# One row of w2 per partition, loaded early in four uneven transfers, in a decode block on one Trainium2 core

## The chip, the core and the metric

The kernel runs on one core of a Trainium2 chip. The core has five engines, each with its own instruction stream: TensorE (PE, with PEld for its weight loads), VectorE (DVE), ScalarE (ACT), GpSimd (POOL) and SyncE (SP), and 16 DMA engines that carry bytes from HBM into SBUF. The metric is the device time of one launch in microseconds (us).

## The reference

Two tokens (B = 2, one each) of width D = 512 pass through an attention part and a feed-forward part, both modulated by a condition `c`:

```python
mod = (_silu(c) @ w_mod).reshape(c.shape[0], 6, 1, -1)
sa, ca, ga, sb, cb, gb = (mod[:, 0], ..., mod[:, 5])
h = _layernorm(x) * (1 + ca) + sa
x = x + ga * _A_ref(h, k_cache, v_cache, wq, wo)   # 32 query heads, 8 KV heads, the last 4096 positions
h = _layernorm(x) * (1 + cb) + sb
x = x + gb * _B_ref(h, w1, w2)                     # silu(h @ w1) @ w2, w1 512x1792, w2 1792x512
```

Everything is float32. The last line's second product, `silu(...) @ w2`, is what the change touches.

## The kernel before, in words

All large inputs are streamed once from HBM into three buffers (`slot[0..2]`, 16384 floats per partition each) by loads on SyncE's queue, in this order: `w_mod`, `wq`, then the four K and four V pieces of the caches alternately, then `wo` in two loads, `w1` in one, and `w2` in four. A load starts as soon as the buffer it writes has been given free; the instructions are put down once, in program order, and a helper (`Flow`) adds the semaphore waits from the regions that instructions read and write. All instructions therefore stand under one line, L117, in the profile. Each load has a semaphore of its own. On each DMA engine the packets of one queue are worked off in the order in which the loads were issued.

`w2` has 1792 rows of 512. Partition p holds rows 14p to 14p+13 (T2 = 14), so "row q" below means 128 rows of the matrix, one per partition, 2 KB in each. `load_rows` loads rows lo to hi of every partition in one transfer: rows 0-7 (2048 KB), 8-11 (1024 KB), 12 and 13 (256 KB each).

The end of the kernel (lines 672 to 713): 64 products make the hidden layer in two halves; VectorE and ScalarE turn each half into `uT` (transpose, scale, silu). Then follow, on TensorE:

- the wide products: rows 0-7, each one product over all 512 columns, four side by side in the partitions of bank D (`product`); ScalarE copies the sum to `wide`;
- the narrow products: for each further row, four products of 128 columns into `y` (`narrow`), rows 8-11; then the copied wide sum, added through `id4` by the same helper; then rows 12 and 13.

VectorE scales `y` by `gb` and adds `x1`, and SyncE stores the result.

## Time and profile before

| | us |
|---|---|
| median of 3 runs (lowest, highest) | 234.55 (234.53, 234.64) |
| the profiled execution, its own time | 234.44 |
| its span, first to last instruction | 233.1 |
| busy: PE, DVE, ACT, POOL | 161.0, 107.5, 32.5, 7.3 |
| bytes read | 97.53 MB, 418 GB/s over the span |

The span is shorter than the time by what lies before the first and after the last instruction. A row of the timeline gives start, length, engine, line, operation, output<-inputs, form and count, and in brackets the idle time before it with what ended it. The chain of work that ended last goes back from the last instruction, at each step to what released it. For a load, the time from its issue to its landing is given; issue plus that time is when an engine waiting for it can go on. The DMA share is the mean busy share of the 16 DMA engines: one engine alone is 0.06.

### The profile page before, as it was taken

The page shows a single profiled execution, that of the slowest core. Times are in us where ns is not written, and L with a number is a line of the kernel's source. Part 1 is how long each engine was busy: PE and PEld are TensorE (multiplying, and loading weights), DVE is VectorE, ACT ScalarE, POOL GpSimd, SP SyncE. Part 2 cuts the span into 40 slices and gives each one's busy share as a digit, 9 for nine tenths or more (in the row PEclk, how much of TensorE's full clock was granted, in tenths as well). Part 3 has the DMA queues.
Part 4 walks back from the last instruction along what each step waited for, and adds up shares of the span by engine and source line. Part 5 has one row for each costly group of instructions (what it writes and reads, how often), then busy time and mean ns, then how long its engine had stood idle before and what let it go on. Part 6 is the DMA issues. An engine that isn't in the chain of part 4 may idle for free.

```text
span 233.1 us, 2459 instructions
## 1 busy us (share of the span) xinstructions
PE 161.0 (69%) x1086; PEld 43.8 (19%) x1086; DVE 107.5 (46%) x137; ACT 32.5 (14%) x57; POOL 7.3 (3%) x26
## 2 busy tenths in 40 slices
PE   0013906920699479989669989829998937989965
PEld 0002201210000011023300023310002422543332
DVE  6014130131999699833099924049965010020351
ACT  2003010010000244021400021140003050010501
POOL 4000000000000000000000000000000030000000
PEclk9999985775599979999979999988999997999999
DMA  7998998989989898899989999899998989989992
GB/s 270 473 518 360 416 484 360 531 371 472 416 371 529 371 507 374 382 506 394 498 371 416 472 405 486 382 472 416 405 475 382 507 354 413 498 346 442 421 403 90
DMA packets 2494, 97.68 MB, mean 419 GB/s; under 512 B 284, under 2 KB 308, under 8 KB 564
## 3 DMA queue, kind: packets, MB, share of 16 engines
q1 hardware_dynamic: 2460, 97.52, 97.2%
q8 instruction: 8, 0.13, 0.2%
q14 instruction: 2, 0.02, 0.0%
q10 hardware_dynamic: 24, 0.01, 0.0%
HBM read 97.53 MB, written 0.00 MB: 418 GB/s over the span
## 4 chain that ended last, share of the span: by engine, by line
DMA 49%; DVE 26%; PE 19%; another core or an unknown queue 3%; issue 1%; ACT 1%; SPq 0%; POOL 0%
DVE store L117 24%; DMA store<-in_A_k_cache_dram 17%; DMA store<-in_B_w_dram 16%; DMA store<-in_A_wq_dram 15%; PE bankD L117 13%; PE bankA L117 3%; DVE mx L117 2%; PE bankC L117 1%; PE bankO L117 1%; PE bankB L117 1%; ACT store L117 1%; SPq L117 0%; DVE qbd L117 0%; DVE mg L117 0%
## 5 line engine op out<-in xcount | busy, mean ns | idle before, releaser
L117 DVE STREAM_TRANSPOSE store<-store 128x2048 f32<-128x2048 f32 (+2 forms) x40 | 77.1, 1981 | 33.6 <-DMA store<-in_A_k_cache_dram 27.9
L117 PE MATMUL bankA<-store,qbd 128*16 128x512 f32 x256 | 64.5, 1082 | 24.6 <-DVE store L117 23.0
L117 PE MATMUL bankD<-store,ptb 128*32 128x256 f32 (+1 forms) x384 | 45.0, 461 | 4.2 <-DMA store<-in_A_v_cache_dram 4.2
L117 PE MATMUL bankD<-store 128*32 128x512 f32 x176 | 23.2, 677 | 10.0 <-DMA store<-in_A_wq_dram 8.0
L117 PEld LDWEIGHTS bankD<-store,ptb 128*32 128x32 f32 (+1 forms) x384 | 17.3, 121 | 32.6 <-issue 24.1
L117 PE MATMUL bankB<-store 128*32 128x256 f32 (+3 forms) x72 | 7.2, 471 | 20.6 <-DVE store L117 20.6
L117 PEld LDWEIGHTS bankA<-store,qbd 128*16 128x16 f32 x256 | 4.6, 97 | 76.4 <-DVE store L117 75.9
L117 ACT COPY bias<-bankB 128x1 f32<-128x1 f32 x4 | 0.6, 159 | 85.7 <-PE bankB L117 85.7
L117 PEld LDWEIGHTS bankD<-store 128*32 128x32 f32 x176 | 6.8, 124 | 25.6 <-issue 22.1
L117 ACT ACTIVATE ptb<-bankC,par 128x512 f32<-128x512 f32 x16 | 11.0, 688 | 3.1 <-PE bankC L117 2.7
L117 ACT COPY store<-bankD 128x512 f32<-128x512 f32 (+1 forms) x7 | 3.9, 558 | 48.8 <-PE bankD L117 48.8
L117 DVE TENSOR_REDUCE mx<-bankA 128x1 f32<-128x1024 f32 x4 | 4.9, 1225 | 8.7 <-PE bankA L117 8.7
L117 PEld LDWEIGHTS bankB<-store 128*32 128x32 f32 (+1 forms) x72 | 3.9, 149 | 24.1 <-DVE store L117 22.2
L117 DVE RECIPROCAL store<-bankB 128x2 f32<-128x2 f32 x1 | 0.2, 171 | 17.1 <-PE bankB L117 17.1
L117 POOL MEMSET store<- 128x128 f32 (+3 forms) x11 | 3.2, 293 | 137.9 <-PE bankD L117 118.2
L117 PE MATMUL bankC<-qbd,store 128*128 128x512 f32 x14 | 7.3, 626 | 0.0
L117 DVE STREAM_TRANSPOSE store<-bankD 128x512 f32<-128x512 f32 x2 | 1.4, 720 | 12.1 <-PE bankD L117 12.1
L117 DVE STREAM_TRANSPOSE store<-bankA 128x128 f32<-128x128 f32 (+1 forms) x2 | 0.7, 368 | 12.3 <-PE bankA L117 12.3
L117 PE MATMUL bankO<-store,pick 128*64 128x128 f32 x32 | 4.4, 279 | 2.9 <-ACT store L117 2.9
L117 ACT ACT_TABLE_LOAD x4 | 5.1, 1283 | 2.8 <-DVE id L117 2.8
L117 ACT ACTIVATE store<-store,key 128x512 f32<-128x512 f32 x7 | 4.7, 716 | 5.5 <-DVE store L117 5.5
L117 DVE BATCH_NORM_STATS2 store<-x_sp 128x6 f32<-128x128 f32 x1 | 0.3, 295 | 10.7 <-DMA x_sp<-in_A_x_dram 10.7
(79 smaller groups left out, 61.4 us busy)
## 6 DMA issues: line engine op xcount, KB each, us to landing
store<-in_w_mod_dram SPq DMA_DIRECT2D x1, 6144.0 KB, 17.1
store<-in_A_wo_dram SPq DMA_DIRECT2D x1, 6144.0 KB, 33.6
store<-in_B_w_dram SPq DMA_DIRECT2D x1, 3584.0 KB, 31.9
store<-in_A_wo_dram SPq DMA_DIRECT2D x1, 2048.0 KB, 38.1
store<-in_B_w_dram SPq DMA_DIRECT2D x1, 2048.0 KB, 36.5
store<-in_B_w_dram SPq DMA_DIRECT2D x1, 1024.0 KB, 38.5
store<-in_B_w_dram SPq DMA_DIRECT2D x2, 256.0 KB, 38.7
store<-in_A_k_cache_dram SPq DMA_DIRECT2D x4, 33.5
```

What stands on the lines that cost most here:

```text
L117: ins = getattr(eng, method)(*args, **kw)
```

## The change

The last row of each partition (row 13) is no longer the last load. It is loaded right behind `w1`, ahead of all other rows of `w2`, in four transfers that take the partitions 0-50, 51-75, 76-79 and 80-127. The other loads become rows 0-7, 8-10, 11 and 12. The products follow the new order: row 13 comes first among the narrow ones, straight behind the wide products, then rows 8-10, the wide sum, and rows 11 and 12. Their number stays the same.

```diff
     w1t |= load_rows(w1, 4, 0, 4, slot[0], 0)
-    for lo, hi in ((0, 8), (8, 12), (12, 13), (13, 14)):
+
+    w2t[T2 - 1] = slot[0][:, 4 * F + (T2 - 1) * D :][:, :D]
+    for p0, p1 in ((0, 51), (51, 76), (76, 80), (80, P)):
+        sp.dma_start(
+            w2t[T2 - 1][p0:p1], w2.rearrange("(p q) e -> p q e", q=T2)[p0:p1, T2 - 1]
+        )
+    for lo, hi in ((0, 8), (8, 11), (11, 12), (12, 13)):
         w2t |= load_rows(w2, T2, lo, hi, slot[0], 4 * F + lo * D)
...
     act.copy(wide, acc)
-    for tt in range(8, T2 - 2):
-        narrow(y, uT[:, tt, :], w2t[tt], tt == 8, False)
+    narrow(y, uT[:, T2 - 1, :], w2t[T2 - 1], True, False)
+    for tt in range(8, T2 - 3):
+        narrow(y, uT[:, tt, :], w2t[tt], False, False)
     narrow(y, id4, wide, False, False)
-    for tt in range(T2 - 2, T2):
-        narrow(y, uT[:, tt, :], w2t[tt], False, tt == T2 - 1)
+    for tt in range(T2 - 3, T2 - 1):
+        narrow(y, uT[:, tt, :], w2t[tt], False, tt == T2 - 2)
```

## The prediction, made before the changed kernel ran

> **What bounds the kernel now.** I read the page first (span, queues), then the chain of work that ended last, then the timeline of the last 12 us, then the SyncE queue's issues, and last the DMA share in slices of 0.2 us. The page says that one queue moves nearly all bytes and is busy for nearly the whole span:

> ```profile
> span 233.1 us, 2459 instructions
> q1 hardware_dynamic: 2460, 97.52, 97.2%
> q8 instruction: 8, 0.13, 0.2%
> q14 instruction: 2, 0.02, 0.0%
> q10 hardware_dynamic: 24, 0.01, 0.0%
> ```

> The columns after the queue's name are packets, MB and share of 16 engines' span. The kernel is a stream of loads; what an edit at its end can win is only how soon the last arithmetic follows the last bytes. The chain (start, length, what) shows that end:

> ```profile
> 190.38 38.46 DMA store<-in_B_w_dram
> 228.84 0.04 issue
> 228.88 1.78 PE bankA L117 x56
> 230.66 0.02 issue
> 230.69 0.30 DVE store L117
> ```

> The load issued at 190.38 (w2 rows 8-11) lands at 228.84; TensorE then runs 56 instructions with no further wait on the chain, and 2.4 us of fixed work (two VectorE instructions, the store) follow to 233.1. Which landings matter is seen by putting the issues beside their times to landing:

> ```profile
> 189.53 0.33 SPq L117 DMA_DIRECT2D store<-in_B_w_dram  x1
> 189.90 0.91 SPq L117 DMA_DIRECT2D store<-in_B_w_dram  x2
> 190.86 0.46 SPq L117 DMA_DIRECT2D store<-in_B_w_dram  x1
> 191.36 1.11 SPq L117 DMA_DIRECT2D store<-in_B_w_dram  x1
> store<-in_B_w_dram SPq DMA_DIRECT2D x1, 3584.0 KB, 31.9
> store<-in_B_w_dram SPq DMA_DIRECT2D x1, 2048.0 KB, 36.5
> store<-in_B_w_dram SPq DMA_DIRECT2D x1, 256.0 KB, 38.6
> store<-in_B_w_dram SPq DMA_DIRECT2D x1, 256.0 KB, 38.7
> ```

> So w1 lands at 189.53+31.9 = 221.4, rows 0-7 at 189.90+36.5 = 226.4, row 12 at 190.86+38.6 = 229.46, row 13 at 191.36+38.7 = 230.06. TensorE against these:

> ```profile
> 225.22 0.18 DVE L117 TENSOR_TENSOR store<-store 128x14 f32<-128x14 f32 x1
> 226.49 2.03 PE L117 MATMUL bankD<-store 128*32 128x512 f32 x16 [1.73 <-DVE store L117]
> 227.24 0.18 DVE L117 TENSOR_TENSOR store<-store 128x14 f32<-128x14 f32 x1
> 228.56 0.59 ACT L117 COPY store<-bankD 128x512 f32<-128x512 f32 x1 [1.84 <-PE bankD L117]
> 228.88 1.08 PE L117 MATMUL bankA<-store 128*32 128x128 f32 x32 [0.36 <-DMA store<-in_B_w_dram]
> 229.78 0.40 PE L117 MATMUL bankA<-store,id 128*32 128x128 f32 x8
> 230.00 0.62 PE L117 MATMUL bankA<-store 128*32 128x128 f32 x16
> ```

> The wide products start at 226.49. The trace names VectorE as their releaser, but its instruction was over at 225.40; what ended last is the landing of rows 0-7 at 226.4. Then TensorE stands for 0.36 us until rows 8-11 are there. Row 13 lands at 230.06, before TensorE reaches it (its 8 instructions are the last of the 16 from 230.00), so the very last transfer isn't what ends the kernel: **two waits do, 226.4 for rows 0-7 and 228.84 for rows 8-11**.

> The third thing is how evenly the 16 engines finish (columns: window, its length, busy time of PE, PEld, DVE, ACT and POOL with counts, clock, DMA share, GB/s):

> ```profile
> 227.50:227.70 0.20, 0.20 (x8) 0.11 (x2) 0.00 (x0) 0.00 (x0) 0.00 (x0) 1.00 1.00 399
> 227.70:227.90 0.20, 0.20 (x7) 0.00 (x0) 0.00 (x0) 0.00 (x0) 0.00 (x0) 1.00 0.63 246
> 227.90:228.10 0.20, 0.20 (x8) 0.00 (x0) 0.00 (x0) 0.00 (x0) 0.00 (x0) 1.00 0.52 195
> 228.30:228.50 0.20, 0.20 (x4) 0.00 (x0) 0.00 (x0) 0.00 (x0) 0.00 (x0) 1.00 0.66 256
> 228.70:228.90 0.20, 0.02 (x3) 0.02 (x3) 0.00 (x0) 0.20 (x1) 0.00 (x0) 1.00 0.54 205
> 228.90:229.10 0.20, 0.20 (x8) 0.20 (x12) 0.00 (x0) 0.20 (x1) 0.00 (x0) 1.00 0.53 205
> 229.10:229.30 0.20, 0.20 (x16) 0.20 (x12) 0.00 (x0) 0.05 (x1) 0.00 (x0) 1.00 0.35 133
> 229.30:229.50 0.20, 0.20 (x18) 0.20 (x12) 0.00 (x0) 0.00 (x0) 0.00 (x0) 1.00 0.17 62
> q8 instruction: 1, 0.02, 10.6%
> q14 instruction: 1, 0.01, 1.0%
> ```

> All 16 are busy until 227.7; about 10 (0.66) at 228.4, 8 or 9 (0.53) at 229.0, none soon after 229.5. So six engines are through at about 227.8, a couple at about 228.7, eight between 229.1 and 229.5. The last two rows say why: one code fetch (q8) in a window of 0.6 us held 10.6% of 16 engines, 1.02 us of one engine, and there are eight of them; one q14 packet in a window of 2 us held 1.0%, 0.32 us, and there are two. Eight engines late by 1.3 to 1.7 us, two by less, six by nothing: the counts fit.

> **The change part by part.** *How four odd transfers are spread.* The queue rows can be counted out: 2460 = 17 loads x (128 rows + 16 completions) + 12 for the store, and 24 = 2 x (8 rows + 4 completions) for the two loads whose outermost dimension is 4. A load over 128 goes to 16 engines in shares of 8, one over 4 to four engines in shares of 2; every row that there is shows equal shares. For 51, 25, 4 and 48 partitions no row exists. The ends are 3, 5, 4 and 16 engines (equal shares: 51 = 3x17, 25 = 5x5) and, at the other end, nearly 16 each. I take equal shares, the only kind in the rows, and that each load begins at the same first engine: three engines get 17+5+1+3 = 26 rows, the fourth 9, the fifth 8, eleven get 3 (78+9+8+33 = 128), where each had 8. [...] By unequal shares the sum would be that of the even rival below.

> *Price of a 2 KB row on one engine:* eight rows per engine lie between 229.46 and 230.06: 0.60/8 = 0.075; between rows 8-11 and row 12, 0.62/8 = 0.078. I take 0.077.

> *What moves.* Row 13 (all 128 partitions) now sits ahead of rows 0-7 in every engine's queue. Rows 0-7 come later by 3 x 0.077 = 0.23 us on eleven engines and by 26 x 0.077 = 2.0 us on three. At the end of the stream the eleven are 5 x 0.077 = 0.39 us earlier, the three 18 x 0.077 = 1.39 us later. w1 stands ahead of all this and keeps 221.4.

> *TensorE.* 14 rows of products before and after, the same instruction count; row 13's eight now come straight behind the wide products, with no wait since it landed long ago, and cover the 0.36 us gap. From the start of the wide products the work is 2.03+1.78 = 3.81 us if nothing overlaps; it is less, since consecutive groups overlap (the group at 229.78 starts 0.18 before the one before it ends at 229.96) and the second half of the wide products needs a VectorE result of 227.42, past which they now start. I use 3.5, with 3.8 as the other end.

> *Waits and issues.* Three more loads on SyncE's queue cost it 0.33 to 1.11 us each; behind them stand only later loads, needed some 37 us on, and the output store after TensorE's end, so that is the cover. Row 13 needs four waits on TensorE instead of one; its instructions queue behind wide products of 2.03 us, which hide them (by the chain's 0.04 us after a landing, 0.16 us uncovered). The copy of the wide sum (0.59 us) has four rows' products between it and its use, as before; they took 1.08-0.18 = 0.90 us, so it stays hidden though they now start with it.

> *The sum* hangs on which three engines are first. If one of them is of the middle group (0.8 us ahead of the last), it has rows 0-7 at about 226.4-0.8+2.0 = 227.6, and the wide products start at 227.7. End of TensorE 227.7+3.5 = 231.2 (3.8: 231.5) instead of 230.66: +0.54 to +0.84; I take +0.6, near the end that the overlap shows. Rows 8-10 (three quarters of 2.44 us, 1.83) land at 229.4, row 12 at 230.7, both just ahead of need. The profiled execution took 234.44 us, 0.11 under the median shown: 234.44+0.6 = 235.04, and 235.1 on the median's scale.

> **Rivals.**
> *Clean three (not slower).* All three are of the six: rows 0-7 land there at 226.4-1.7+2.0 = 226.7, on the eleven at 226.63; start 226.8, end 230.3 to 230.6: -0.36 to -0.06, so 234.2 to 234.5. It decides once the three are 1.7 us ahead. For it: six such engines exist. Against: no view names an engine; followed packet by packet (each starts as its predecessor on that engine ends), two of the four engines that carried ScalarE's small loads seem to have had the q14 packets. That tilts me to the middle group. No more than this can be won: every engine gets three rows ahead of rows 0-7.

> *Even spread (the change does nothing of its kind).* Eight rows on each engine: rows 0-7 at 226.4+0.62 = 227.0, start 227.1, end 230.6 to 230.9: 0 to +0.25, 234.5. Against: equal shares in the counts.

> *A late engine among the three.* One of the eight that had a 1.02 us fetch: rows 0-7 at 226.0 to 226.4+2.0, start 228.1 to 228.5, end 231.6 to 232.0: +0.95 to +1.35, 235.5 to 236.0. By mere count likely (eight of 16); against it the same tracking.

> *Shared write path.* A 26-row share covers at least 18 partitions that other engines write at the same moment with their own loads. If a partition's path takes one engine's rate, such a row costs up to twice: 18 x 0.077 = 1.39 us more at most, half of it 0.7. On top of the forecast +1.3 to +2.0, so 235.8 to 236.5. In the trace 16 engines never cross: no row shows it either way. [...]

> **How the numbers follow.** Forecast 0.38, clean 0.20, even 0.12, late engine 0.16, shared path 0.14. Bounds of 0.2% (0.47 us) are about what a measurement here can tell. Faster by that needs more than the clean case's -0.36: 0.06, for what I may have missed. Same: the rest of clean (0.14), even (0.12), the forecast's lower edge (0.14): 0.40. Slower: 0.24+0.16+0.14 = 0.54. The range runs from 234.1 (clean) to 236.2, leaving out part of the shared path; the forecast's own is 234.8 to 235.4.

> **What would show it.** Wide products later than 226.49 (227.7 by the forecast, 226.8 if clean) show the three's load; narrow work right behind them, without a 0.36 us gap, shows the cover. DMA share: eleven engines done 0.4 us earlier and three left alone past 229.6 (0.19 of 16) is the forecast; a sharp common end is the clean case; packets of 2 KB much over 0.077 us in 219 to 223 the shared path. The prediction is wrong if the wide products start before 226.9 or after 228.1.

## The result, and the profile after

The changed kernel takes 237.06 us (median of 6 runs, 236.20 to 237.77) against 234.60 before: ratio 1.0105, interval 1.0085 to 1.0124. It is slower, by more than the 235.1 forecast and beyond the range's 236.2. The six times lie at two levels, 236.20 to 236.44 and 237.69 to 237.77, three each. The profiled execution is one of the upper ones (237.76 us).

From the page of the changed kernel, its span and the queue that carries the loads:

```profile
span 236.4 us, 2465 instructions
q1 hardware_dynamic: 2616, 97.52, 96.6%
```

Its chain of waits (start, length, what):

```profile
191.56 37.09 DMA store<-in_B_w_dram
228.66 0.14 issue
228.79 3.52 PE bankD L117 x16
232.31 1.61 PE bankA L117 x56
```

And the last part of its timeline:

```profile
222.57 1.74 PE L117 MATMUL bankA<-store 128*32 128x224 f32 x32 [1.28 <-DMA store<-in_B_w_dram]
228.31 0.18 DVE L117 TENSOR_TENSOR store<-store 128x14 f32<-128x14 f32 x1
228.79 3.52 PE L117 MATMUL bankD<-store 128*32 128x512 f32 x16 [2.95 <-DMA store<-in_B_w_dram]
232.13 1.06 PE L117 MATMUL bankA<-store 128*32 128x128 f32 x32
233.26 0.62 PE L117 MATMUL bankA<-store 128*32 128x128 f32 x16
```

The load that ends the chain is now rows 0-7, issued at 191.56: it lands at 228.66, 2.3 us after the 226.4 of before, and the wide products wait for it (VectorE's last result, 1.07 us later than before since w1 is late too, is there at 228.49 and doesn't decide). They then take 3.52 us instead of 2.03. Behind them the narrow work follows without the old gap of 0.36 us, as it was meant to. The sum: 2.30 (start 228.79 for 226.49) + 1.49 (wide products) - 0.36 (gap) - 0.17 (the chain counts 1.61 for the narrow work and not 1.78) = 3.26 us, from 230.66 to 233.92; the times differ by 237.76-234.44 = 3.32. Two things need a cause: 2.3 us of landing and 1.5 us of wide products.

The windows of the kernel before, from the time at which the first engines are through with w1 (columns as in the prediction: the last three are TensorE's granted clock, DMA share and GB/s):

```profile
219.50:221.00 1.50, 1.50 (x4) 0.38 (x2) 0.65 (x3) 1.30 (x2) 0.00 (x0) 1.00 1.01 431
221.00:222.00 1.00, 0.54 (x13) 0.38 (x16) 0.00 (x0) 0.00 (x0) 0.00 (x0) 1.00 1.04 442
222.00:223.00 1.00, 1.00 (x28) 0.66 (x24) 0.00 (x0) 0.00 (x0) 0.00 (x0) 1.00 1.00 426
```

The same windows of the changed kernel, and two later ones for the clock:

```profile
219.50:221.00 1.50, 1.50 (x4) 0.49 (x3) 0.65 (x3) 1.47 (x2) 0.00 (x0) 1.00 1.04 299
221.00:222.00 1.00, 0.30 (x1) 0.00 (x0) 0.00 (x0) 0.07 (x1) 0.00 (x0) 1.00 1.21 291
222.00:223.00 1.00, 0.43 (x11) 0.30 (x15) 0.00 (x0) 0.00 (x0) 0.00 (x0) 1.00 0.92 272
...
225.90:228.70 2.80, 0.00 (x0) 0.00 (x0) 2.07 (x10) 0.21 (x1) 0.00 (x0) 0.99 0.95 385
228.70:230.40 1.70, 1.61 (x8) 0.46 (x12) 0.00 (x0) 0.00 (x0) 0.00 (x0) 0.50 0.79 310
```

The engines are as busy as before (share about 1) and move a third less: 272 to 299 GB/s where it was 426 to 442. They aren't idle, their packets are slow. The trace keeps every packet's start, length and size, and these records say the same: 16 KB packets that begin in 221 to 222 take 1.01 to 1.14 us, where before they take 0.61 to 0.62; 2 KB packets of row 13 have medians of 0.115, 0.127 and 0.145 us in the three windows, where the same row in the even kernel below takes 0.084. Long 2 KB packets are the sign that the prediction named for the shared write path. And the clock is 0.50 under the wide products, right after a stretch of 2.8 us in which TensorE did nothing.

### The profile page after: what moved, and what is told of

It is laid out like the page before. It is cut to its first block, busy times and chain, and to the rows that moved or that the text cites. A ratio compares the mean times of both kernels' runs of the same rounds, so it can differ in the third digit from the quotient of the medians.

```text
span 236.4 us, 2465 instructions
## 1 busy us (share of the span) xinstructions
PE 162.6 (69%) x1086; PEld 43.9 (19%) x1086; DVE 107.5 (45%) x137; ACT 32.6 (14%) x57; POOL 7.4 (3%) x26
## 3 DMA queue, kind: packets, MB, share of 16 engines
q1 hardware_dynamic: 2616, 97.52, 96.6%
## 4 chain that ended last, share of the span: by engine, by line
DMA 47%; DVE 26%; PE 20%; another core or an unknown queue 3%; SPq 1%; issue 1%; ACT 1%; POOL 0%
DVE store L117 24%; DMA store<-in_A_k_cache_dram 17%; DMA store<-in_B_w_dram 16%; DMA store<-in_A_wq_dram 15%; PE bankD L117 13%; PE bankA L117 3%; DVE mx L117 2%; PE bankC L117 1%; PE bankO L117 1%; SPq L117 1%; PE bankB L117 1%; ACT store L117 1%; DVE qbd L117 0%; DVE mg L117 0%
## 5 line engine op out<-in xcount | busy, mean ns | idle before, releaser
L117 DVE STREAM_TRANSPOSE store<-store 128x2048 f32<-128x2048 f32 (+2 forms) x40 | 77.1, 1981 | 35.0 <-DMA store<-in_A_k_cache_dram 29.3
L117 PE MATMUL bankA<-store,qbd 128*16 128x512 f32 x256 | 65.0, 1089 | 25.5 <-DVE store L117 23.7
L117 PE MATMUL bankD<-store,ptb 128*32 128x256 f32 (+1 forms) x384 | 45.6, 464 | 3.9 <-DMA store<-in_A_v_cache_dram 3.9
L117 PE MATMUL bankD<-store 128*32 128x512 f32 x176 | 24.0, 701 | 10.5 <-DMA store<-in_A_wq_dram 7.6
L117 PEld LDWEIGHTS bankD<-store,ptb 128*32 128x32 f32 (+1 forms) x384 | 17.4, 121 | 32.9 <-issue 24.3
L117 PE MATMUL bankB<-store 128*32 128x256 f32 (+3 forms) x72 | 7.2, 472 | 20.6 <-DVE store L117 20.6
L117 PEld LDWEIGHTS bankA<-store,qbd 128*16 128x16 f32 x256 | 4.7, 97 | 77.6 <-DVE store L117 77.1
L117 ACT COPY bias<-bankB 128x1 f32<-128x1 f32 x4 | 0.6, 159 | 87.0 <-PE bankB L117 87.0
L117 ACT ACTIVATE ptb<-bankC,par 128x512 f32<-128x512 f32 x16 | 11.0, 689 | 3.0 <-PE bankC L117 2.6
L117 PEld LDWEIGHTS bankD<-store 128*32 128x32 f32 x176 | 6.4, 128 | 26.5 <-issue 22.1
L117 ACT COPY store<-bankD 128x512 f32<-128x512 f32 (+1 forms) x7 | 3.9, 559 | 51.6 <-PE bankD L117 51.6
L117 DVE TENSOR_REDUCE mx<-bankA 128x1 f32<-128x1024 f32 x4 | 4.9, 1225 | 8.7 <-PE bankA L117 8.7
L117 PEld LDWEIGHTS bankB<-store 128*32 128x32 f32 (+1 forms) x72 | 4.0, 151 | 24.1 <-DVE store L117 22.2
L117 DVE RECIPROCAL store<-bankB 128x2 f32<-128x2 f32 x1 | 0.2, 171 | 17.4 <-PE bankB L117 17.4
L117 POOL MEMSET store<- 128x128 f32 (+3 forms) x11 | 3.2, 295 | 139.2 <-PE bankD L117 118.1
L117 PE MATMUL bankC<-qbd,store 128*128 128x512 f32 x14 | 7.3, 626 | 0.0
L117 DVE STREAM_TRANSPOSE store<-bankA 128x128 f32<-128x128 f32 (+1 forms) x2 | 0.7, 368 | 12.8 <-PE bankA L117 12.8
L117 PE MATMUL bankO<-store,pick 128*64 128x128 f32 x32 | 4.3, 279 | 2.9 <-ACT store L117 2.9
L117 DVE STREAM_TRANSPOSE store<-bankD 128x512 f32<-128x512 f32 x2 | 1.4, 719 | 10.4 <-PE bankD L117 10.4
L117 ACT ACTIVATE store<-store,key 128x512 f32<-128x512 f32 x7 | 4.7, 717 | 5.5 <-DVE store L117 5.5
L117 DVE BATCH_NORM_STATS2 store<-x_sp 128x6 f32<-128x128 f32 x1 | 0.3, 294 | 10.8 <-DMA x_sp<-in_A_x_dram 10.8
## 6 DMA issues: line engine op xcount, KB each, us to landing
store<-in_B_w_dram SPq DMA_DIRECT2D x1, 3584.0 KB, 32.7
store<-in_A_wo_dram SPq DMA_DIRECT2D x1, 2048.0 KB, 37.9
store<-in_B_w_dram SPq DMA_DIRECT2D x1, 2048.0 KB, 37.1
store<-in_B_w_dram SPq DMA_DIRECT2D x2, 256.0 KB, 35.7
```

The source lines that it names most:

```text
L117: ins = getattr(eng, method)(*args, **kw)
```

## The experiments

**Even.** Row 13 early, in one transfer over all partitions (the page's 2604 packets are 2460 + 128 rows + 16 completions, as for the other full-width loads).

```diff
-    for p0, p1 in ((0, 51), (51, 76), (76, 80), (80, P)): ...
+    w2t |= load_rows(w2, T2, T2 - 1, T2, slot[0], 4 * F + (T2 - 1) * D)
```

> The changed kernel with row 13 in one transfer of 128 partitions, still right behind w1: eight rows on every engine, each written by the engine that writes these partitions in all other loads. Theory A (three engines overloaded, nothing else): the overload is gone, rows 0-7 land at 226.4+0.62 = 227.0, wide products start near 227.1, time 234.4 to 234.8. Theory B (partitions share a write path between engines): no crossing is left either, so the same 234.4 to 234.8, and 16 KB packets at one length. Theory C (a row ahead of rows 0-7 is itself what costs): still above 236.

234.41 to 236.47 us in 10 runs (ratio 1.0043, 1.0022 to 1.0063), again two levels: four at 234.41 to 234.96, six at 236.07 to 236.47. Its windows, in the profiled execution (an upper one):

```profile
219.50:221.00 1.50, 1.48 (x4) 0.38 (x2) 0.63 (x3) 1.25 (x1) 0.00 (x0) 1.00 1.00 410
221.00:222.00 1.00, 0.52 (x12) 0.39 (x16) 0.00 (x0) 0.00 (x0) 0.00 (x0) 1.00 1.14 471
222.00:223.00 1.00, 1.00 (x28) 0.65 (x24) 0.00 (x0) 0.00 (x0) 0.00 (x0) 1.00 1.04 442
```

And its wide products in the timeline:

```profile
227.14 2.83 PE L117 MATMUL bankD<-store 128*32 128x512 f32 x16 [2.35 <-DMA store<-in_B_w_dram]
```

The rate is back at 410 to 471 GB/s, and the wide products start at 227.14, 0.65 us later than before, near the 0.62 that eight rows cost by the price of 0.077. So the early row itself isn't the cause: the lower level is the kernel before's time. No theory had foreseen the upper level; its number alone would fit theory C, and the fillers below rule that out.

**Cross.** The same, in three transfers of 48, 48 and 32 partitions: 16 completions each (2636 packets are 2460 + 128 + 3 x 16), so by equal shares still eight rows on each engine, but other partitions.

```diff
-    for p0, p1 in ((0, 51), (51, 76), (76, 80), (80, P)):
+    for p0, p1 in ((0, 48), (48, 96), (96, P)):
```

> The changed kernel with row 13 in three transfers of 48, 48 and 32 partitions: 3, 3 and 2 rows on every engine, so eight each as in the even kernel, but mostly in partitions that other engines write in the other loads. Theory A: as the even kernel, 234.4 to 234.8. Theory B: packets of w1 and of rows 0-7 beside them lengthen, rows 0-7 land 0.5 to 1.4 us after the even kernel's, time 235.0 to 236.2, or 1.5 more if TensorE's clock drops on the wide products. Theory C: above 236, as the even kernel.

236.04, 237.84, 237.85 and 237.98 us; ratio 1.0121 (1.0091 to 1.0151). Its windows:

```profile
219.50:221.00 1.50, 1.50 (x6) 0.86 (x6) 0.64 (x3) 1.10 (x2) 0.00 (x0) 1.00 0.97 264
221.00:222.00 1.00, 0.67 (x2) 0.00 (x0) 0.00 (x0) 0.45 (x1) 0.00 (x0) 1.00 1.17 320
222.00:223.00 1.00, 0.23 (x7) 0.18 (x11) 0.00 (x0) 0.00 (x0) 0.00 (x0) 1.00 1.06 311
```

Its wide products:

```profile
228.98 3.52 PE L117 MATMUL bankD<-store 128*32 128x512 f32 x16 [2.92 <-DMA store<-in_B_w_dram]
```

264 to 320 GB/s and the wide products at 228.98, 1.84 us after the even kernel's, with no engine overloaded if the shares are equal. This is the changed kernel's loss, without its unevenness.

**Uneven last.** The kernel before, row 13 last, but in the change's four transfers.

```diff
-    for lo, hi in ((0, 8), (8, 12), (12, 13), (13, 14)): ...
+    for lo, hi in ((0, 8), (8, 12), (12, 13)): ...
+    for p0, p1 in ((0, 51), (51, 76), (76, 80), (80, P)): ...   # row 13
```

> The kernel before with its own order (row 13 last), but row 13 in the four transfers of 51, 25, 4 and 48 partitions. Theory A: the first three engines take 18 rows more at the end, one of them 0.6 to 0.9 us behind the clean ones, so row 13 lands at 230.3 to 230.7 instead of 230.06, time 234.7 to 235.2. Theory B: while the others finish rows 8-12 the three cross their partitions, up to 1.4 us more: row 13 at 231 to 232, time 235.5 to 236.5. Theory C: no row moved ahead, 234.5.

235.28 to 235.71 us, ratio 1.0036 (1.0022 to 1.005), one level. Three of the four times are between the two theories' ranges, the fourth in theory B's, and the place is another than both said: it is rows 8-11 that come late. That engines which are through then write into partitions of those that still load them is the author's reading; the trace names no engine. The narrow work begins at 229.77 instead of 228.88, by its timeline:

```profile
221.92 1.74 PE L117 MATMUL bankA<-store 128*32 128x224 f32 x32 [0.46 <-DMA store<-in_B_w_dram]
226.93 2.02 PE L117 MATMUL bankD<-store 128*32 128x512 f32 x16 [1.74 <-DVE store L117]
229.77 1.08 PE L117 MATMUL bankA<-store 128*32 128x128 f32 x32 [0.82 <-DMA store<-in_B_w_dram]
```

In this trace at most about half of these 0.89 us can be the crossing's: the products of w1 (221.92 for 221.50) and the wide products (226.93 for 226.49) start 0.42 and 0.44 us late already, ahead of any crossing, for a reason that stays open, and 0.45 us are left. The rate is down from 227 on, in its windows:

```profile
227.00:228.00 1.00, 1.00 (x12) 0.45 (x16) 0.60 (x3) 0.14 (x1) 0.00 (x0) 1.00 0.86 274
228.00:229.00 1.00, 0.94 (x8) 0.04 (x2) 0.00 (x0) 0.02 (x1) 0.00 (x0) 1.00 0.71 244
```

where the kernel before, at the same share, has

```profile
227.00:228.00 1.00, 1.00 (x16) 0.33 (x8) 0.39 (x2) 0.00 (x0) 0.00 (x0) 1.00 0.87 346
```

**After with fillers, even with fillers.** Filler products in TensorE's idle stretch: three in the changed kernel, two in the even one.

```diff
+    for i in range(3):          # 2 in the even kernel
+        fill(512)
     ax, x1 = later(P), later(P)
```

> The changed kernel with three more filler products (2.6 us of TensorE) behind the products of w1, in the stretch in which it stood idle from 225.8 to 228.8. Theory D (the granted clock halves after a stretch with little TensorE work, and that makes the two levels of the changed kernel's times): no half clock on the wide products, they take 2.0 us and not 3.5, all runs 236.1 to 236.5. Against it (the halving comes by itself): times still at two levels, 236.3 and 237.7.

235.89 to 236.39 us in 5 runs (ratio 1.0067, 1.0053 to 1.0081): the upper level is gone. The same in the even kernel:

> The even kernel (row 13 in one transfer of 128 partitions behind w1) with two filler products in TensorE's idle stretch of 2.35 us ahead of the wide products. Theory D (the clock halves because TensorE stood idle): only one level of times, that of the even kernel's undisturbed executions, 234.4 to 234.9; wide products 2.0 us. Against it: two levels, 234.5 and 236.2, as without the fillers. Against the kernel before: 0.999 to 1.001, since its 0.36 us gap is covered and rows 0-7 are 0.62 us later.

234.41 to 234.94 in 11 runs, ratio 1.0001 (0.9992 to 1.001): one level, and the kernel before's time. The changed kernel's timeline with its fillers (bank C) ahead of the wide products:

```profile
226.10 2.84 PE L117 MATMUL bankC<-qbd,store 128*128 128x512 f32 x6
228.88 1.92 PE L117 MATMUL bankD<-store 128*32 128x512 f32 x16
231.75 0.62 PE L117 MATMUL bankA<-store 128*32 128x128 f32 x16
```

The wide products of the even kernel with fillers:

```profile
227.41 1.92 PE L117 MATMUL bankD<-store 128*32 128x512 f32 x16 [0.30 <-DVE store L117]
```

The wide products take 1.92 us in both, and theory D holds: the upper level comes from the clock.

**Home and foreign.** These settle whether it is overload, the reading or the writing. Eight loads of four partitions each, ahead of rows 0-7; only the written partitions differ. These kernels, and the two after them, leave out rows 8-13 of all other partitions, and `Flow` is told that each of the eight loads writes one partition only, since the ranges it notes would overlap. So packets and waits are compared, and not the times (one run each: 239.52 us home, 242.86 foreign, 240.56 one engine, 243.49 near). Which engine writes which partitions stands in no record: in the four expectations from here on it is the author's assumption, and home, foreign and crossing are named by it. Measured are rates, waits and packet times.

```diff
+    for p in (0, 1, 2, 3, 32, 33, 34, 35):
+        sp.dma_start(tail[p + AT : p + AT + 13 : 4],      # AT = 0 home, 64 foreign, 4 near
+                     w2.rearrange("(p q) e -> p (q e)", q=T2)[p : p + 13 : 4, 8 * D :])
+    w2t |= load_rows(w2, T2, 0, 8, slot[0], 4 * F)
```

> The kernel before without the loads of rows 8-13 as a whole; instead eight loads of four partitions each (12 KB per partition, step 4) stand ahead of rows 0-7, in partitions 0-15 and 32-47. This leaves rows 8-13 of the other partitions unloaded, so the time is not to be compared, only the packets. By the four-way split four engines get 96 KB more each, 3.6 us at 0.46 us per 12 KB, and by the way the other loads are spread they write only partitions that are theirs in all other loads too. Theory A (only overload counts): twelve engines untouched, rows 0-7 land there by 226.4, on the four at 228 to 229.1; bytes per us in 219.5 to 223 stay near 425. Theory B (shared write path): the same here, since nothing crosses.

> The same eight loads from the same rows of w2 on the same four engines, but written to partitions 64-79 and 96-111, which four other engines write in all other loads; rows 8-13 otherwise unloaded, as in the home kernel. Theory A: no difference to the home kernel, 425 GB/s. Theory B: eight of 16 engines go at about half rate while this lasts: 300 to 340 GB/s in 219.5 to 223, w1 lands 0.5 to 1.5 us later than in the home kernel, and rows 0-7 land at 230 to 232.5 on the four, 1.5 to 3.5 us after the home kernel's.

The windows of the home kernel:

```profile
219.50:221.00 1.50, 1.50 (x4) 0.47 (x3) 0.65 (x3) 1.48 (x2) 0.00 (x0) 1.00 0.98 418
221.00:222.00 1.00, 0.54 (x9) 0.20 (x12) 0.00 (x0) 0.05 (x1) 0.00 (x0) 1.00 1.03 438
222.00:223.00 1.00, 1.00 (x28) 0.67 (x24) 0.00 (x0) 0.00 (x0) 0.00 (x0) 1.00 0.97 414
```

Its w1 and wide products:

```profile
221.74 1.74 PE L119 MATMUL bankA<-store 128*32 128x224 f32 x32 [0.46 <-DMA store<-in_B_w_dram]
229.54 3.64 PE L119 MATMUL bankD<-store 128*32 128x512 f32 x16 [4.53 <-DMA store<-in_B_w_dram]
```

The windows of the foreign kernel:

```profile
219.50:221.00 1.50, 1.50 (x4) 0.38 (x2) 0.65 (x3) 1.37 (x2) 0.00 (x0) 1.00 1.30 279
221.00:222.00 1.00, 0.11 (x1) 0.00 (x0) 0.00 (x0) 0.00 (x0) 0.00 (x0) 1.00 0.71 147
222.00:223.00 1.00, 0.00 (x0) 0.00 (x0) 0.00 (x0) 0.00 (x0) 0.00 (x0) 1.00 1.02 213
```

Its w1 and wide products:

```profile
223.43 2.86 PE L119 MATMUL bankA<-store 128*32 128x224 f32 x32 [2.32 <-DMA store<-in_B_w_dram]
233.90 3.64 PE L119 MATMUL bankD<-store 128*32 128x512 f32 x16 [5.54 <-DMA store<-in_B_w_dram]
```

The same eight transfers (both pages count 2092 packets: 14 x 144 + 12 + 8 x (4 rows + 4 completions)), the same bytes and source rows: 414 to 438 GB/s at home, 147 to 279 in foreign partitions, and the wide products 4.4 us later. So it is neither the overload nor the reading; it is where the bytes are written. The loss is larger than theory B said (300 to 340 GB/s): each load has four completions, so four engines are taken to carry it, and yet not only the packets of the eight concerned slow down. By the packet records all 30 packets of 16 KB that begin in 221 to 224.5 take 1.22 to 1.27 us; at home 74 of 75 take 0.61 to 0.62. The wide products wait for rows 0-7 and start at 229.54 and 233.90, later than both expectations had these rows (228 to 229.1 and 230 to 232.5).

**One engine, and near.** How far the damage reaches: one load of 17 partitions, which by its single completion one engine carries (its page's 2046 packets are 14 x 144 + 12 + 17 rows + 1), and the foreign loads shifted by 4 partitions instead of 64.

```diff
-    for p in (0, 1, 2, 3, 32, 33, 34, 35): ...
+    sp.dma_start(tail[64:81, : 3 * D], w2.rearrange("(p q) e -> p (q e)", q=T2)[64:81, 8 * D : 11 * D])
```

> As the home and foreign kernels, but one load of 17 partitions (64 to 80, 6 KB each) stands ahead of rows 0-7: 17 has no divisor up to 16 but 1, so one engine carries 102 KB, 3.9 us alone, into partitions that five other engines write. Rows 8-13 of the rest stay unloaded, so only the packets count. Theory B1 (one path per group of partitions, only the two engines on it share): at any moment two of 16 engines go at half rate, 390 GB/s or more in 221 to 224.5, other engines' 16 KB packets at 0.61 us. Theory B2 (a crossing holds up all engines, as in the foreign kernel, where every packet took twice its time): 210 to 300 GB/s, all 16 KB packets near 1.2 us, for about twice 3.9 us.

> The foreign kernel with its eight loads written four partitions on from home (4 to 19 and 36 to 51) instead of 64: each of four engines writes its neighbour's partitions, and three of the four engines so met are themselves among the four. Theory B1: the sharing is between five engines, 16 KB packets of the other eleven at 0.61 us, about 360 to 400 GB/s in 221 to 224.5. Theory B2: as the foreign kernel, 150 to 220 GB/s and 1.2 us for all. If it is the distance of 64 partitions and not the sharing that costs: as the home kernel, 410 to 440.

The stretch that the two expectations name, in the home kernel, the one-engine kernel and the near kernel, in this order:

```profile
221.00:224.50 3.50, 3.04 (x61) 1.83 (x64) 0.88 (x3) 0.05 (x1) 0.00 (x0) 1.00 0.98 414
221.00:224.50 3.50, 2.98 (x61) 1.92 (x64) 0.89 (x4) 0.00 (x0) 0.00 (x0) 1.00 0.99 374
221.00:224.50 3.50, 2.33 (x45) 1.35 (x48) 0.20 (x1) 0.11 (x1) 0.00 (x0) 1.00 1.01 370
```

The near kernel ahead of it:

```profile
219.50:221.00 1.50, 1.50 (x5) 0.52 (x4) 0.65 (x3) 1.44 (x2) 0.00 (x0) 1.00 0.92 249
```

One crossing engine costs the stream a tenth, 374 GB/s for 414: below B1's 390, far above B2's 300. In the packet records of 221 to 224.5 three 16 KB packets took 1.0 us or more and the others 0.62 to 0.74, where 0.61 is usual, so all are touched, mildly. The crossing packets of 6 KB themselves took 0.34 to 0.53 us, where packets of 6 KB take 0.23 in the even kernel. Near has 370 in the named stretch, within B1's 360 to 400, but 249 ahead of it, where the home kernel has 418; a distance of 64 partitions isn't needed. Neither theory holds alone.

## Why the prediction was wrong

*The spread over engines* was right in what the runs show of it. The page's 2616 packets are 2460 + 128 rows + 28 completions, and 28 = 3+5+4+16, the numbers of engines that were assumed. Which engines these are, no count shows, nor that the four transfers begin at the same one, which is how three engines come to 26 rows.

*What bounds the end* was right: the landing of rows 0-7, then TensorE without a pause. The 0.36 us gap went, as said.

*The price of a row, 0.077 us on one engine,* is the step that failed. It was read from rows sent over all 128 partitions, eight to an engine, and was used for 26 rows on one engine, which by the shares taken mostly lie in partitions that others load. The even kernel shows the price holding for the plain transfer (wide products 0.65 us later for eight rows, 0.62 by the price), the cross kernel what crossing adds with no overload: 1.84 us. The changed kernel's rows 0-7 came 2.3 us late where the forecast had 1.2, and the wide products started at 228.79, past the 228.1 that the prediction gave as its limit. That step also let w1 keep its 221.4, because it stands ahead in each queue; its products started at 222.57, and before at 221.50:

```profile
221.50 1.74 PE L117 MATMUL bankA<-store 128*32 128x224 f32 x32 [0.46 <-DMA store<-in_B_w_dram]
```

In the even kernel they start at 221.48. So w1's place ahead of row 13 in the queue did not protect it here: it came 1.07 us later with row 13 in four transfers behind it, and no later with row 13 in one.

*The shared write path* was among the rivals, as a surcharge of at most 1.39 us, with a chance of 0.14, because no row showed it. Its 235.8 to 236.5 holds the lower level, 236.20 to 236.44, in part by luck: it priced the crossing rows alone, and in the run the 16 KB packets of the loads beside them took up to 1.14 us as well. For some such sharing speak the home and foreign kernels, 414 to 438 GB/s against 147 to 279 with nothing changed but the partitions written; which partitions share what, no run shows, and that the home partitions are their engines' own was the author's assumption.

*The overload of three engines* carried the forecast, and by these runs adds little to the crossing: the cross kernel, with none, is at 236.04 and 237.84 to 237.98, as slow as the changed one. In the home kernel, the 384 KB that go ahead of rows 0-7 on four engines left the others alone: 16 KB packets stayed at 0.61 to 0.62 us. The prediction's sign for overload, three engines left alone past 229.6, isn't there in the changed kernel: the DMA share is still 0.80 from 229.9 to 230.1 and 0.61 from 230.3 to 230.5, then 0.05 to 0.11 from 230.7 to 231.3, one or two engines.

*TensorE's clock* was in no case. The prediction took 3.5 us for the wide and narrow products; in the changed kernel with fillers, whose wide products took 1.92 us, they take that (228.88 to 232.37), and with the wide products at clock 0.50 they took 3.52+1.61. It is why half of the runs lie 1.4 us higher, and the fillers remove it. A wait for data was priced as its length alone, without what it does to the engine that waits. In the traces the clock goes to 0.50 by windows of 3.41 us with little TensorE work (the last section). A window needn't be idle throughout for it: one with TensorE busy for 0.60 of 3.41 us was enough here.

Together, on the scale of the profiled execution: 235.04 forecast, +1.09 for the wide products' start (228.79 for 227.7), 236.13, near the lower level; +1.63 for the clock (3.52+1.61 for 3.5), 237.76, the upper.

## What to carry to other kernels

Splitting the early row into transfers of fewer partitions did not pay here: by equal shares the even and cross kernels move the same number of rows per engine, and the crossing one costs 1.4 to 1.7 us more, lower level against lower (236.04 in one run, 234.41 to 234.96) and upper against upper (about 237.9, 236.07 to 236.47). When a load is split by hand, measure it against the plain transfer over 128 partitions, which here held 410 to 471 GB/s from 219.5 to 223 where three transfers of 48, 48 and 32 had 264 to 320. And when a change makes TensorE wait longer than about 1.9 us (an estimate; the last section works it out), put filler products there before judging it: for the even kernel, with 2.35 us of wait, they were the difference between medians of 236.08 and 234.66 us.

## What the runs showed that was not expected

Crossing slows packets that take no part in it: in the foreign kernel, with loads of four completions each, the rate fell to 147 to 213 GB/s from 221 to 223, a third to a half of the home kernel's 414 to 438, and every 16 KB packet of 221 to 224.5 took twice its time (1.22 to 1.27 us for 0.61 to 0.62); with the load of one completion the rate was 374 from 221 to 224.5. Why the damage spreads is open.

```profile
225.24:228.65 3.41, 0.60 (x16) 0.13 (x4) 2.42 (x12) 0.43 (x2) 0.00 (x0) 1.00 0.96 392
224.61:228.02 3.41, 1.06 (x13) 0.37 (x13) 2.15 (x10) 0.30 (x2) 0.00 (x0) 1.00 0.96 386
224.09:227.51 3.42, 1.69 (x28) 0.66 (x24) 2.49 (x12) 0.43 (x2) 0.00 (x0) 1.00 0.98 398
228.65:232.07 3.42, 3.28 (x16) 0.90 (x20) 0.00 (x0) 0.00 (x0) 0.00 (x0) 0.50 0.45 175
```

TensorE was busy for 0.60 and 1.06 us of 3.41 ahead of half clock, and for 1.69 in the kernel before, which kept its clock. An estimate from these numbers: a window must hold about 1.9 us of idle time (55% of 3.41). If the windows fall by chance, one of them gets that much of a 2.35 us stretch in 0.6 of the executions, of a 2.95 us stretch in 0.8, and of 1.73 us never; at the upper level were 6 of 10, 3 of 6 and none of 37.
